# V loads on the scalar engine's DMA queue, K loads on the sync engine's

## The chip, the cores and the metric

The kernel runs on one core of a Trainium2 chip. The metric is the time of one launch in microseconds (us) of device time. A span is the time from the first to the last instruction in a profile; the launch time is about 1.7 to 1.8 us longer in every profiled run but one (198.7 against 200.4 us for the kernel before; the exception, LEAD = 1, is named below).

The engines are called PE (matmul), DVE (vector), ACT (scalar), POOL (GpSimd) and SP (sync). SP and ACT can both issue DMA transfers; SPq and ACTq in the profile are those issues.

## The reference

One step of attention with cached keys and values, one query token per sequence, over the last W = 512 positions of the cache:

```
B, D, Hq, Hkv, Sk, Dh = 32, 512, 32, 8, 2048, 128        # bf16
q = (x @ wq)                                             # 32 heads of 128
k, v = the last W = 512 positions of k_cache, v_cache, each of the 8 kv heads repeated 4 times
p = softmax(q k^T * Dh**-0.5)
out = (p v) @ wo                                         # [32, 1, 512]
```

Bytes: K and V are 33.55 MB each, wq and wo 4.19 MB each; together 75.5 MB. The unit of this document is a *batch*: the K, or the V, of one sequence is 1.05 MB, loaded as two transfers of 512 KB.

## The kernel before

All loads are issued by SP, so they go through one queue, in this order (shortened):

```python
NK = 6; NV = 8; LEAD = 5; PVLAG = 6
# SP
x, then wq in 4 pieces
for b in range(B + LEAD):
    if b < B:
        load_k(b)            # waits until the K buffer of batch b-6 was transposed
    if b >= LEAD:
        load_v(b - LEAD)     # waits until PV of batch b-LEAD-8 is done
sp.wait_ge(pe_qt, 1)         # wo takes the place of wq
wo in 4 pieces of 8 heads
# ...
```

PE does, at step `it`: the 32 transposes of K(it), the scores of batch it-1, and PV (probabilities times V) of batch it-6. After every fourth batch there is a softmax: max on DVE, exp on ACT, normalising on DVE, transposes of P on PE, copies of them on ACT. ACT also copies a quarter of each transposed K. At the end comes the output projection, piece by piece as wo lands:

```python
pe.wait_ge(dve_oT, B)                       # all 32 PV results copied
for hq in range(HQ):
    c = hq % 4
    if hq % 8 == 0:
        pe.wait_ge(sem_wo[hq // 8], 16)
    ins = pe.matmul(KT_ps[:, c, :].bitcast(F32)[32 * c:32 * (c + 1), :],
                    lhsT=oT_sb[:, :, hq], rhs=wo_sb[:, hq, :], ...)
# then DVE and ACT copy the four partial sums, one matmul adds them, ACT copies, SP stores
```

Of the kernel before, what the change touches and what calls it, by code (L numbers as in the profile page):

```python
# [7 lines left out]
ACTF = mybir.ActivationFunctionType  # L8
# [4 lines left out]
def bass_standalone__sliding_block_cached__sampling_kernel(  # L13
# [7 lines left out]
):  # L21
    B, Sq, D = x.shape
    _, HKV, SK, DH = k_cache.shape
    HD = wq.shape[1]
    HQ = HD // DH
# [12 lines left out]
    NV = 8  # L38
    NKT = 3
    NQB = 8  # L40
    LEAD = 5
# [3 lines left out]
    with ExitStack() as es:  # L45
        sb = lambda name, shape, dt: es.enter_context(nc.sbuf_tensor(name, shape, dt))
        ps = lambda name, shape, dt: es.enter_context(nc.psum_tensor(name, shape, dt))
        sem = lambda name: es.enter_context(nc.semaphore(name))
# [5 lines left out]
        V_sb = sb("V_sb", [P, NV, 2, NR, DH], BF16)  # L54
# [18 lines left out]
        junk = sb("junk", [P, 2], F32)  # L73
# [10 lines left out]
        sem_v = [sem(f"sem_v{i}") for i in range(NV)]  # L84
# [6 lines left out]
        pe_PV = sem("pe_PV")  # L91
# [17 lines left out]
        act_PT = sem("act_PT")  # L109
        act_out = sem("act_out")  # L110
        act_warm = sem("act_warm")
        pool_init = sem("pool_init")
        pool_qbd = sem("pool_qbd")
        block = es.enter_context(nc.Block())
# [4 lines left out]
        def cache_rows(cache, b, h):  # L119
            return cache[b, 4 * h:4 * h + 4, SK - W:, :].rearrange("g (s r) d -> s g (r d)", s=NS)  # L120

        @block.sync
        def _(sp):
            sp.dma_start(x_sb[:, :], x.rearrange("b s d -> b (s d)")).then_inc(sem_x, 16)
            for kt in range(DKT):
                sp.dma_start(wq_sb[:, kt, :], wq[kt * P:(kt + 1) * P, :]).then_inc(sem_wq[kt], 16)  # L126

            def load_k(b):
                if b >= NK:
                    sp.wait_ge(pe_T[3], b - NK + 1)  # L130
                for h in range(2):
                    sp.dma_start(  # L132
                        K_sb[:, b % NK, h].rearrange("p r d -> p (r d)"), cache_rows(k_cache, b, h)
                    ).then_inc(sem_k[b % NK][h], 16)

            def load_v(b):
                if b >= NV:
                    sp.wait_ge(pe_PV, b - NV + 1)
                for h in range(2):
                    sp.dma_start(  # L140
                        V_sb[:, b % NV, h].rearrange("p r d -> p (r d)"), cache_rows(v_cache, b, h)
                    ).then_inc(sem_v[b % NV], 16)

            for b in range(B + LEAD):
                if b < B:
                    load_k(b)
                if b >= LEAD:
                    load_v(b - LEAD)
            sp.wait_ge(pe_qt, 1)
            for c in range(4):  # L150
                sp.dma_start(  # L151
                    wo_sb[:, c * 8:(c + 1) * 8, :],
                    wo[c * 1024:(c + 1) * 1024, :].rearrange("(h d) n -> d h n", d=P),
                ).then_inc(sem_wo[c], 16)
            sp.wait_ge(act_out, 1)
            sp.dma_start(out.rearrange("b s d -> b (s d)"), out_sb[:, :]).then_inc(sem_out, 16)
            sp.wait_ge(sem_out, 16)
# [228 lines left out]
        @block.scalar  # L386
        def _(act):
            act.wait_ge(pool_init, 3)
            act.activation(junk[:, 1:2], junk[:, 0:1], ACTF.Exp).then_inc(act_warm, 1)
            act.wait_ge(pe_qt, 1)  # L390
            act.activation(
                QT_sb[:, 16:32, :].rearrange("p h b -> p (h b)"), PT_ps[:, 1, :].bitcast(F32), ACTF.Copy
            ).then_inc(act_qt, 1)

            def kt_evac(b):
                if b >= NKT:
                    act.wait_ge(pe_S, b - NKT + 1)
                act.wait_ge(pe_T[3], b + 1)
                act.activation(  # L399
                    KT_sb[:, b % NKT, 1, 8:16, :, :], KT_ps[:, 3, :], ACTF.Copy  # L400
                ).then_inc(act_T, 1)

            def do_exp(q):
                act.wait_ge(dve_sm, 2 * q + 2)
                if q >= 1:
                    act.wait_ge(dve_P, 4 * q)
                act.activation(  # L407
                    P_f32[:, :], S_ps[:, :], ACTF.Exp,
                    bias=negmax[:, q:q + 1], scale=SCALE, accum_out=sums[:, q:q + 1],
                ).then_inc(act_exp, 1)  # L410

            def pt_evac(q):
                if q >= 2:
                    act.wait_ge(pe_PV, 4 * (q - 2) + 4)
                for i in range(2):
                    act.wait_ge(pe_PT, 2 * q + i + 1)
                    act.activation(  # L417
                        PT_sb[:, q % 2, 8 * i:8 * i + 8, :].rearrange("p r n -> p (r n)"),
                        PT_ps[:, i, :], ACTF.Copy,
                    ).then_inc(act_PT, 1)  # L420

            for it in range(B + 2):
                if it < B:
                    kt_evac(it)
                if it % 4 == 0 and 4 <= it:
                    do_exp((it - 4) // 4)
                if it % 4 == 1 and 5 <= it:
                    pt_evac((it - 5) // 4)
            act.wait_ge(pe_fin, 1)
            for c in range(2, 4):  # L430
                act.activation(
                    X_sb[32 * c:32 * (c + 1), :], KT_ps[:, c, :].bitcast(F32)[32 * c:32 * (c + 1), :], ACTF.Copy
                ).then_inc(act_x, 1)
            act.wait_ge(pe_out, 1)
            act.activation(out_sb[:, :], QO_ps[0:32, :], ACTF.Copy).then_inc(act_out, 1)
# [28 lines left out]
```

## Time and profile before

| | before |
|---|---|
| time, median of 4 runs | 200.36 us (200.28 to 200.49) |
| span of the profiled run | 198.7 us |
| DMA rate, 20 to 160 us (table of windows) | 408 GB/s |
| K(31) has landed, its last transposes start | 166.05 us |
| last copy of a PV result ends | 183.84 us |
| last piece of wo has landed, its matmuls start | 192.86 us |

These lines are from the page of the kernel before: the span; the busy time of each engine; two rows of the table of 40 slices of 5 us (DMA busy in tenths, GB/s); the one data queue with its share of the 16 DMA engines; the chain of waits by engine; and three kinds of issue, with the median time from issue to landing at the end of the line.

```profile
span 198.7 us, 5891 instructions
...
PE 142.8 (72%) x2597; PEld 111.8 (56%) x2597; DVE 100.8 (51%) x188; ACT 58.3 (29%) x70; POOL 13.3 (7%) x46
...
DMA  5999999999999999999999999999999999999930
GB/s 181 424 418 411 409 407 412 403 411 407 408 411 403 409 407 407 410 407 409 406 407 410 407 413 403 408 407 407 411 406 411 401 409 406 410 396 334 344 133 7
...
q1 hardware_dynamic: 23264, 75.57, 96.6%
...
SPq 50%; DMA 28%; PE 14%; DVE 3%; issue 2%; ACT 1%; DVEq 0%
...
K_sb<-in_k_cache_dram SPq DMA_DIRECT2D x64, 512.0 KB, 15.6
V_sb<-in_v_cache_dram SPq DMA_DIRECT2D x64, 512.0 KB, 15.4
...
w_sb<-in_wo_dram SPq DMA_DIRECT2D x4, 1024.0 KB, 17.6
```

The transfers bound the kernel. From the second slice to the 35th they run at some 400 to 425 GB/s and the DMA row shows 9 tenths, while PE is busy 72% and DVE 51%. The chain is made of SP's issues and of landings. A transfer lands 15.6 us after its issue (median) because others are in front of it: 11 in the median had been issued and had not landed.

These lines are from the timeline of the last 35 us: start, duration, engine, line, operation, output and inputs, count, and in brackets the idle time before it and what ended that.

```profile
166.05 1.75 PE L236 MATMUL KT_ps<-perm,K_sb 128*128 128x128 bf16 x16 [0.35 <-DMA K_sb<-in_k_cache_dram]
...
183.65 0.19 DVE L366 CAST oT_sb<-QO_ps 128x32 bf16<-128x32 f32 x1 [1.11 <-PE QO_ps L286]
...
184.35 1.07 PE L308 MATMUL KT_ps<-w_sb,oT_sb 128*32 128x512 bf16 x8 [0.73 <-DMA w_sb<-in_wo_dram]
...
192.86 1.08 PE L308 MATMUL KT_ps<-w_sb,oT_sb 128*32 128x512 bf16 x8 [1.61 <-DMA w_sb<-in_wo_dram]
193.99 1.20 ACT L431 ACTIVATE X_sb<-KT_ps 32x512 bf16<-32x512 f32 x2 [15.38 <-PE KT_ps L308]
194.00 1.39 DVE L382 CAST X_sb<-KT_ps 32x512 bf16<-32x512 f32 x2 [10.15 <-PE KT_ps L308]
...
196.72 0.36 SPq L156 DMA_DIRECT2D out_dram<-out_sb  x1
```

There are two chains at the end. One is the *compute tail*: K(31) lands at 166.05 us, and 17.8 us later, at 183.84 us, the last PV result has been copied. The other is the *load tail*: V(27..31) and wo, still in the queue, keep landing until 192.86 us. The second ends later, so it sets the time; PE waits for each piece of wo. After it, a matmul group of 1.08 us and the copies, the adding matmul and the store end the span, 5.8 us in all.

### The profile page before, as it was taken

The page shows a single profiled execution, that of the slowest core. Times are in us where ns is not written, and L with a number is a line of the kernel's source. Part 1 is how long each engine was busy: PE and PEld are TensorE (multiplying, and loading weights), DVE is VectorE, ACT ScalarE, POOL GpSimd, SP SyncE. Part 2 cuts the span into 40 slices and gives each one's busy share as a digit, 9 for nine tenths or more (in the row PEclk, how much of TensorE's full clock was granted, in tenths as well). Part 3 has the DMA queues.
Part 4 walks back from the last instruction along what each step waited for, and adds up shares of the span by engine and source line. Part 5 has one row for each costly group of instructions (what it writes and reads, how often), then busy time and mean ns, then how long its engine had stood idle before and what let it go on. Part 6 is the DMA issues. An engine that isn't in the chain of part 4 may idle for free.

```text
span 198.7 us, 5891 instructions
## 1 busy us (share of the span) xinstructions
PE 142.8 (72%) x2597; PEld 111.8 (56%) x2597; DVE 100.8 (51%) x188; ACT 58.3 (29%) x70; POOL 13.3 (7%) x46
## 2 busy tenths in 40 slices
PE   0448996797787799759776977697769697647431
PEld 0337874776565568556755666566656485537000
DVE  0004579755853577335943595359435944531002
ACT  2001345333252325204522343233423251130003
POOL 8202000000000001000000000000000000000000
PEclk9999999699999969988998799969996797855555
DMA  5999999999999999999999999999999999999930
GB/s 181 424 418 411 409 407 412 403 411 407 408 411 403 409 407 407 410 407 409 406 407 410 407 413 403 408 407 407 411 406 411 401 409 406 410 396 334 344 133 7
DMA packets 23289, 75.95 MB, mean 382 GB/s; under 512 B 2208, under 2 KB 6368, under 8 KB 22752
## 3 DMA queue, kind: packets, MB, share of 16 engines
q1 hardware_dynamic: 23264, 75.57, 96.6%
q8 instruction: 21, 0.34, 0.7%
q14 instruction: 4, 0.03, 0.0%
HBM read 75.53 MB, written 0.03 MB: 380 GB/s over the span
## 4 chain that ended last, share of the span: by engine, by line
SPq 50%; DMA 28%; PE 14%; DVE 3%; issue 2%; ACT 1%; DVEq 0%
SPq L132 24%; DMA K_sb<-in_k_cache_dram 23%; SPq L140 18%; PE KT_ps L236 9%; SPq L151 7%; DMA w_sb<-in_wo_dram 6%; PE S_ps L253 2%; DVE P_ex L359 2%; PE QO_ps L286 1%; SPq L126 1%; DVE KT_sb L337 1%; PE PT_ps L268 1%; PE KT_ps L308 1%; ACT P_f L407 0%; DVEq L45 0%
## 5 line engine op out<-in xcount | busy, mean ns | idle before, releaser
L236 PE MATMUL KT_ps<-perm,K_sb 128*128 128x128 bf16 x1024 | 75.8, 238 | 22.6 <-DMA K_sb<-in_k_cache_dram 22.4
L337 DVE COPY KT_sb<-KT_ps 128x1024 bf16<-128x1024 bf16 x96 | 63.7, 687 | 53.2 <-PE KT_ps L236 52.9
L236 PEld LDWEIGHTS KT_ps<-perm,K_sb 128*128 128x128 bf16 x1024 | 67.0, 107 | 29.2 <-DMA K_sb<-in_k_cache_dram 26.7
L399 ACT ACTIVATE KT_sb<-KT_ps 128x1024 bf16<-128x1024 bf16 x32 | 32.8, 1024 | 83.0 <-PE KT_ps L236 83.0
L286 PEld LDWEIGHTS QO_ps<-PT_sb,V_sb 128*128 128x128 bf16 x1024 | 28.2, 98 | 17.4 <-issue 13.9
L286 PE MATMUL QO_ps<-PT_sb,V_sb 128*128 128x16 bf16 x1024 | 31.2, 171 | 2.4 <-ACT PT_sb L417 1.2
L359 DVE TENSOR_SCALAR P_ex<-P_f,recip 32x512 bf16<-32x512 f32 x32 | 25.3, 791 | 1.1
L253 PE MATMUL S_ps<-KT_sb,QBD 128*32 128x512 bf16 x256 | 22.7, 437 | 0.0
L417 ACT ACTIVATE PT_sb<-PT_ps 128x1024 bf16<-128x1024 bf16 x16 | 15.5, 1021 | 19.1 <-PE PT_ps L268 19.1
L268 PE MATMUL PT_ps<-ident,P_ex 128*128 128x128 bf16 x128 | 9.7, 236 | 10.6 <-DVE P_ex L359 10.6
L196 POOL COPY QBD<-QT_sb 128x32 bf16<-128x32 bf16 x32 | 7.9, 261 | 117.6 <-PE S_ps L253 108.6
L268 PEld LDWEIGHTS PT_ps<-ident,P_ex 128*128 128x128 bf16 x128 | 8.2, 106 | 11.5 <-DVE P_ex L359 11.5
L366 DVE CAST oT_sb<-QO_ps 128x32 bf16<-128x32 f32 x32 | 5.9, 183 | 9.5 <-PE QO_ps L286 9.4
L214 PE MATMUL PT_ps<-xT_sb,w_sb 128*128 128x32 bf16 x128 | 4.1, 188 | 7.6 <-DMA w_sb<-in_wq_dram 7.6
L308 PE MATMUL KT_ps<-w_sb,oT_sb 128*32 128x512 bf16 x32 | 4.3, 637 | 6.0 <-DMA w_sb<-in_wo_dram 6.0
L214 PEld LDWEIGHTS PT_ps<-xT_sb,w_sb 128*128 128x128 bf16 x128 | 3.7, 104 | 8.0 <-DMA w_sb<-in_wq_dram 4.6
L343 DVE TENSOR_REDUCE maxv<-S_ps 128x1 f32<-128x512 f32 x8 | 5.5, 691 | 5.2 <-PE S_ps L253 5.2
L407 ACT ACTIVATE P_f<-S_ps,negmax 128x512 f32<-128x512 f32 x8 | 5.5, 688 | 6.8 <-DVE negmax L345 6.8
L382 DVE CAST X_sb<-KT_ps 32x512 bf16<-32x512 f32 x2 | 1.4, 680 | 10.2 <-PE KT_ps L308 10.2
L329 DVE CAST QT_sb<-PT_ps 128x512 bf16<-128x512 f32 x1 | 0.7, 692 | 11.5 <-PE PT_ps L214 11.5
L253 PEld LDWEIGHTS S_ps<-KT_sb,QBD 128*32 128x32 bf16 x256 | 4.0, 97 | 4.0 <-issue 1.6
L308 PEld LDWEIGHTS KT_ps<-w_sb,oT_sb 128*32 128x32 bf16 x32 | 0.9, 149 | 8.7 <-DMA w_sb<-in_wo_dram 7.9
(27 smaller groups left out, 15.2 us busy)
## 6 DMA issues: line engine op xcount, KB each, us to landing
K_sb<-in_k_cache_dram SPq DMA_DIRECT2D x64, 512.0 KB, 15.6
V_sb<-in_v_cache_dram SPq DMA_DIRECT2D x64, 512.0 KB, 15.4
w_sb<-in_wq_dram SPq DMA_DIRECT2D x4, 1024.0 KB, 7.9
w_sb<-in_wo_dram SPq DMA_DIRECT2D x4, 1024.0 KB, 17.6
x_sb<-in_x_dram SPq DMA_DIRECT2D x1, 32.0 KB, 1.7
out_dram<-out_sb SPq DMA_DIRECT2D x1, 32.0 KB, 1.5
```

The lines of the kernel that those rows point to most:

```text
L132: sp.dma_start(K_sb[:, b % NK, h].rearrange("p r d -> p (r d)"), cache_rows(k_cache, b, h)).then_inc(sem_k[b % NK][h], 16)
L140: sp.dma_start(V_sb[:, b % NV, h].rearrange("p r d -> p (r d)"), cache_rows(v_cache, b, h)).then_inc(sem_v[b % NV], 16)
L151: sp.dma_start(wo_sb[:, c * 8:(c + 1) * 8, :], wo[c * 1024:(c + 1) * 1024, :].rearrange("(h d) n -> d h n", d=P),).then_inc(sem_wo[c], 16)
L196: pool.tensor_copy(dst, src).then_inc(pool_qbd, 1)
L236: ins = pe.matmul(KT_ps[:, t, i * 128:(i + 1) * 128], lhsT=K_sb[:, b % NK, h, 8 * (t % 2) + i, :], rhs=perm[:, :, :], start=True, stop=Tru ...
L253: ins = pe.matmul(S_ps[32 * c:32 * c + 32, :], lhsT=QBD[:, b % NQB, g, :], rhs=KT_sb[:, b % NKT, h, :, c, :], start=(j == 0 and h == 0), s ...
L268: ins = pe.matmul(PT_ps[:, r // 8, (r % 8) * 128:(r % 8 + 1) * 128], lhsT=P_ex[:, r, :, :].rearrange("p s g -> p (s g)"), rhs=ident[:, :], ...
L286: ins = pe.matmul(QO_ps[:, 16 * h:16 * h + 16], lhsT=V_sb[:, b % NV, h, r, :], rhs=PT_sb[:, q % 2, r, :].rearrange("p (c n) -> p c n", c=G ...
L337: dve.tensor_copy(KT_sb[:, b % NKT, t // 2, 8 * (t % 2):8 * (t % 2) + 8, :, :], KT_ps[:, t, :]).then_inc(dve_T, 1)
L359: dve.tensor_scalar(P_ex[rows, :, :, c], P_f32[rows, :].rearrange("p (r s) -> p r s", r=NR), recip[rows, q:q + 1], None, op0=ALU.mult,).th ...
L399: act.activation(KT_sb[:, b % NKT, 1, 8:16, :, :], KT_ps[:, 3, :], ACTF.Copy).then_inc(act_T, 1)
L417: act.activation(PT_sb[:, q % 2, 8 * i:8 * i + 8, :].rearrange("p r n -> p (r n)"), PT_ps[:, i, :], ACTF.Copy,).then_inc(act_PT, 1)
```

## The change

The intent is to spread the issues over two queues: SP issues K, ACT issues V, so that neither waits for the other's buffers. The core of the diff:

```diff
-            def load_v(b):
-                ...                                # on SP
-            for b in range(B + LEAD):
-                if b < B:
-                    load_k(b)
-                if b >= LEAD:
-                    load_v(b - LEAD)
+            for b in range(B):
+                load_k(b)
             sp.wait_ge(pe_qt, 1)
+            sp.wait_ge(act_v, 1)                   # wo after the last V was issued
...
+            def load_v(b):                         # on ACT
+                if b >= NV:
+                    act.wait_ge(pe_PV, b - NV + 1)
+                for h in range(2):
+                    act.dma_start(
+                        V_sb[:, b % NV, h].rearrange("p r d -> p (r d)"), cache_rows(v_cache, b, h)
+                    ).then_inc(sem_v[b % NV], 16)
+            load_v(0)
             for it in range(B + 2):
+                if it + 1 < B:
+                    load_v(it + 1)
+                if it == B - 1:
+                    act.activation(junk..., ACTF.Copy).then_inc(act_v, 1)
                 if it < B:
                     kt_evac(it)
```

(Cut: the declaration of `act_v`, and a wait for ACT's own first exp.) Nothing is computed differently and no byte more is moved. What changes besides the issuing engine is the *order*: LEAD, which held V five batches behind K, is gone.

More of the change, by code (lines that the diff above doesn't have):

```diff
@@ L111, in bass_standalone__sliding_block_cached__sampling_kernel @@
         act_warm = sem("act_warm")
+        act_v = sem("act_v")
         pool_init = sem("pool_init")
@@ L134, in load_k @@
                     ).then_inc(sem_k[b % NK][h], 16)
-            def load_v(b):
-                if b >= NV:
-                    sp.wait_ge(pe_PV, b - NV + 1)
-                for h in range(2):
-                    sp.dma_start(
-                        V_sb[:, b % NV, h].rearrange("p r d -> p (r d)"), cache_rows(v_cache, b, h)
-                    ).then_inc(sem_v[b % NV], 16)
-            for b in range(B + LEAD):
-                if b < B:
-                    load_k(b)
-                if b >= LEAD:
-                    load_v(b - LEAD)
+            for b in range(B):
+                load_k(b)
             sp.wait_ge(pe_qt, 1)
+            sp.wait_ge(act_v, 1)
             for c in range(4):
@@ L389, in _ @@
             act.activation(junk[:, 1:2], junk[:, 0:1], ACTF.Exp).then_inc(act_warm, 1)
+            act.wait_ge(act_warm, 1)
             act.wait_ge(pe_qt, 1)
@@ L420, in pt_evac @@
                     ).then_inc(act_PT, 1)
+            def load_v(b):
[6 more added lines that the diff above has]
+            load_v(0)
             for it in range(B + 2):
+                if it + 1 < B:
+                    load_v(it + 1)
+                if it == B - 1:
+                    act.activation(junk[:, 0:1], junk[:, 1:2], ACTF.Copy).then_inc(act_v, 1)
                 if it < B:
```

## The prediction

> **What bounds the kernel now.** The transfers. The slice table shows DMA at 9 tenths from slice 2 to slice 38 and 403 to 413 GB/s in almost every slice from 4 to 34; the page counts 75.95 MB, and the chain of waits is 50% sync-queue issues and 28% DMA. PE is busy 72%, DVE 51%, ACT 29%. PE waits for K tiles before most transposes (49.1 us in the view of K_sb). One queue carries everything in first-in first-out order: K runs LEAD = 5 batches ahead of V, so K(31) is followed by V(27..31) and by wo. In the timeline K(31) has landed at 166.05 us; from there to the last PV copy at 183.84 us is a compute tail of 17.8 us (transposes, scores, softmax, P transposes, four PV steps). It is hidden, because V(27..31) and wo keep the queue busy until about 192.86 us, when the last wo piece lands. From the last wo matmul group's end (193.94) to the end of the span (198.66) are 4.7 us.
>
> **What the change does.**
> - Issue cost. An unblocked 512 KB issue took 0.60 us on the sync queue (the first K issues, 4.1 to 8.7 us); later ones took 1.08 us and up to 3.7 us because about 12 transfers were outstanding (median 15.6 us to landing). That blocking is backpressure, not lost bandwidth, so freeing SP saves nothing. ACT gains about 1.25 us of issue per batch; with 1.02 us of KT copy and about 0.7 us of exp and PT copies (per batch) it has some 3 us of work in a period of 5.13 us (2.10 MB at 409 GB/s). ACT should not become the limit.
> - Bandwidth. The Trainium skill, "DMA: Bandwidth & Descriptors", section "Issuing engines are not separate DMA queues", says both run on the same 16 engines and only issue time is saved. No trace here has two data queues, so it is untested; I expect 405 to 415 GB/s again.
> - Order. The same page, "Queues, rings and completion order", says each engine round-robins between queues by packet. Both streams have 4 KB packets, so while both have work K gets half. V(it+1) is issued when ACT has copied batch it-1, so V is no longer five batches behind K but level with it. This is the change that matters.
>
> **Cost.** Before, K(31) landed after wq 4 + K 32 + V(0..25) 26 = 62 MiB. After, about 31.5 MiB of V precede it: 67.5 MiB, 5.5 MiB = 5.8 MB more, at 407 GB/s 14.2 us later: about 180 us. wo then needs about 12.5 us (334 GB/s in the last slices) and lands near 194. But the compute tail now starts at 180: the last PV copy at about 198, then four wo matmul groups back to back without DMA waits (0.5 + 4 x 1.08 us), then 4.7 us: span about 207.5, time about 209 us. DMA ends before the compute and idles some 10 us at the end. All of the roughly 9 us lies on the critical path; nothing is gained elsewhere.
>
> **What would show it.** Two data queues of about 36 MB each; K landing about 25 to 30 us after issue, V about 8 to 12; DMA rate unchanged; K(31)'s transposes near 180 us; wo matmuls without waits for wo; chain ending through softmax and PV rather than through wo.
>
> **What would make it wrong.** Unequal sharing: if K gets more than half, V lags and K(31) lands earlier (one batch less V saves 2.6 us, at best the old time). Two queues moving bytes faster or slower by 2% (3.5 us either way). ACT blocked by its issues or by waits for PV, delaying KT copies (slower still). V starvation late in the run.
>
> Predicted 209 us, 203 to 214; faster 0.04, same 0.16, slower 0.80.

## The result

| | before | after |
|---|---|---|
| time, median of 4 runs | 200.36 us | 203.19 us (202.91 to 203.54) |
| ratio | | 1.0142 (1.0123 to 1.0161) |
| span of the profiled run | 198.7 us | 201.2 us |
| DMA rate, 20 to 160 us | 408 GB/s | 408 GB/s |
| last transposes of K(31) start | 166.05 us | 176.59 us |
| last PV copy ends | 183.84 us | 193.21 us |
| last piece of wo has landed | 192.8 us | 193.0 us |

A ratio here is the mean time of one kernel's fast runs over that of the other's in the same rounds, so it is not quite the ratio of the medians. The changed kernel is slower by 1.4%: well outside the noise, and less than 2%. The landings are from the trace's completion events.

The same lines of the page after the change:

```profile
span 201.2 us, 5894 instructions
...
PE 142.7 (71%) x2597; PEld 112.4 (56%) x2597; DVE 101.7 (51%) x188; ACT 58.5 (29%) x71; POOL 13.0 (6%) x46
...
DMA  5999999999999999999999999999999999999800
GB/s 191 417 421 409 408 407 409 411 406 411 406 411 406 412 402 405 411 406 415 402 413 405 408 409 409 409 406 407 412 404 406 411 406 410 388 366 349 292 18 7
...
q1 hardware_dynamic: 14048, 42.01, 53.6%
q10 hardware_dynamic: 9216, 33.56, 41.9%
...
DMA 76%; PE 11%; SPq 6%; DVE 3%; ACT 2%; issue 1%; DVEq 0%; ACTq 0%
...
K_sb<-in_k_cache_dram SPq DMA_DIRECT2D x64, 512.0 KB, 27.0
V_sb<-in_v_cache_dram ACTq DMA_DIRECT2D x64, 512.0 KB, 16.4
...
w_sb<-in_wo_dram SPq DMA_DIRECT2D x4, 1024.0 KB, 11.9
```

The busy times are nearly the same (ACT is at 29% as before) and so is the rate. There are two data queues: SP's (q1), with K and the weights, and ACT's (q10), with V. A K transfer now takes 27.0 us from issue to landing instead of 15.6, because it gets only half of the rate. The chain of waits is no longer issues of SP but landings of K.

The timeline of the end, after:

```profile
176.59 1.07 PE L227 MATMUL KT_ps<-perm,K_sb 128*128 128x128 bf16 x16 [0.46 <-DMA K_sb<-in_k_cache_dram]
...
193.02 0.19 DVE L357 CAST oT_sb<-QO_ps 128x32 bf16<-128x32 f32 x1 [1.11 <-PE QO_ps L277]
...
193.26 3.15 PE L299 MATMUL KT_ps<-w_sb,oT_sb 128*32 128x512 bf16 x32 [0.28 <-DVE oT_sb L357]
...
196.47 1.39 DVE L373 CAST X_sb<-KT_ps 32x512 bf16<-32x512 f32 x2 [3.26 <-PE KT_ps L299]
...
198.99 0.36 SPq L147 DMA_DIRECT2D out_dram<-out_sb  x1
```

The load tail has not moved: wo has landed at 193.0 us. The compute tail has: it starts 10.5 us later and now ends after the load tail. So the 32 matmuls with wo, which before were spread over the waits for wo, stand behind the last PV copy in one group of 3.15 us; no wait for wo is left. They end at 196.41 us instead of 193.94, which is the 2.5 us by which the span grew.

### The profile page after: what moved, and what is told of

Read it like the earlier page. It is cut to its first block, busy times and chain, and to the rows that moved or that the text cites. A ratio compares the mean times of both kernels' runs of the same rounds, so it can differ in the third digit from the quotient of the medians.

```text
span 201.2 us, 5894 instructions
## 1 busy us (share of the span) xinstructions
PE 142.7 (71%) x2597; PEld 112.4 (56%) x2597; DVE 101.7 (51%) x188; ACT 58.5 (29%) x71; POOL 13.0 (6%) x46
## 4 chain that ended last, share of the span: by engine, by line
DMA 76%; PE 11%; SPq 6%; DVE 3%; ACT 2%; issue 1%; DVEq 0%; ACTq 0%
DMA K_sb<-in_k_cache_dram 76%; PE KT_ps L227 5%; SPq L133 5%; PE QO_ps L277 3%; PE KT_ps L299 2%; DVE P_ex L350 2%; SPq L127 1%; ACT PT_sb L409 1%; PE S_ps L244 1%; PE PT_ps L259 1%; DVE oT_sb L357 0%; ACT P_f L399 0%; DVEq L45 0%; DVE maxv L334 0%; DVE X_sb L373 0%
## 5 line engine op out<-in xcount | busy, mean ns | idle before, releaser
L227 PE MATMUL KT_ps<-perm,K_sb 128*128 128x128 bf16 x1024 | 77.1, 238 | 33.5 <-DMA K_sb<-in_k_cache_dram 33.0
L328 DVE COPY KT_sb<-KT_ps 128x1024 bf16<-128x1024 bf16 x96 | 64.5, 688 | 61.7 <-PE KT_ps L227 61.3
L277 PEld LDWEIGHTS QO_ps<-PT_sb,V_sb 128*128 128x128 bf16 x1024 | 28.4, 99 | 17.8 <-issue 14.3
L277 PE MATMUL QO_ps<-PT_sb,V_sb 128*128 128x16 bf16 x1024 | 31.3, 171 | 2.4 <-ACT PT_sb L409 1.2
L244 PE MATMUL S_ps<-KT_sb,QBD 128*32 128x512 bf16 x256 | 23.5, 451 | 0.0
L383 ACT ACTIVATE QT_sb<-PT_ps 128x512 bf16<-128x512 f32 x1 | 0.6, 598 | 12.3 <-PE PT_ps L205 12.3
L436 ACT ACTIVATE X_sb<-KT_ps 32x512 bf16<-32x512 f32 x2 | 1.2, 590 | 8.5 <-PE KT_ps L299 8.5
L299 PE MATMUL KT_ps<-w_sb,oT_sb 128*32 128x512 bf16 x32 | 3.2, 562 | 0.3 <-DVE oT_sb L357 0.3
## 6 DMA issues: line engine op xcount, KB each, us to landing
V_sb<-in_v_cache_dram ACTq DMA_DIRECT2D x64, 512.0 KB, 16.4
```

The source lines that it names most:

```text
L227: ins = pe.matmul(KT_ps[:, t, i * 128:(i + 1) * 128], lhsT=K_sb[:, b % NK, h, 8 * (t % 2) + i, :], rhs=perm[:, :, :], start=True, stop=Tru ...
L244: ins = pe.matmul(S_ps[32 * c:32 * c + 32, :], lhsT=QBD[:, b % NQB, g, :], rhs=KT_sb[:, b % NKT, h, :, c, :], start=(j == 0 and h == 0), s ...
L277: ins = pe.matmul(QO_ps[:, 16 * h:16 * h + 16], lhsT=V_sb[:, b % NV, h, r, :], rhs=PT_sb[:, q % 2, r, :].rearrange("p (c n) -> p c n", c=G ...
L328: dve.tensor_copy(KT_sb[:, b % NKT, t // 2, 8 * (t % 2):8 * (t % 2) + 8, :, :], KT_ps[:, t, :]).then_inc(dve_T, 1)
```

## The experiments

Theory A: what counts is how far K is ahead of V in the bytes moved. It fixes when K(31) lands and so when the compute tail starts; the compute tail costs time only where it ends later than the load tail. Which engine issues is of no account. Rival B: the V issues on ACT delay the copies of K. Rival C: two data queues disturb each other.

### Two queues, V later: act_lag and act_late

```diff
# act_lag: against the changed kernel
-            load_v(0)
             for it in range(B + 2):
-                if it + 1 < B:
-                    load_v(it + 1)
+                if 1 <= it <= B:
+                    load_v(it - 1)
...
             sp.wait_ge(act_v, 1)
+            sp.wait_ge(sem_v[29 % NV], 32 * (29 // NV + 1))    # wo after V(29) has landed

# act_late: against the changed kernel
+            act.wait_ge(sem_k[2][1], 16)                       # K(2) has landed
             load_v(0)
```

> V stays on the scalar queue with the same issues, but two batches later: V(b-1) instead of V(b+1) at the scalar engine's step b; wo is held until V(29) has landed, so that it does not take half the rate from V at the end. Theory A (what counts is how many batches of V have been moved when K(31) lands, whichever queue moves them): V starts to flow near 24 us instead of 18.7, K(31) lands at 165 to 170 us instead of 176.5, the last PV copy is over before 190 us, and the time is that of the kernel before, 200.4 +- 0.8 us. Theory B (issues on the scalar engine, 1.2 us per batch, slow the copies): 203 us as in the changed kernel. Theory C (two data queues disturb each other): 203 us as well.

> The changed kernel with one wait more: the scalar engine waits for K(2) to land before it issues V(0); from then on every V(b+1) is issued at the same program step as in the changed kernel. Theory A with a conserved lead (both queues always have work and share equally, so the lead that K has when V starts lasts to the end): V starts to flow about 4 to 5 us later, K's lead grows by about one batch or more and K(31) lands about 3 to 5 us earlier, 172 to 174 us; time 200.4 to 201.5 us. Rival A2 (the program step at which V is issued sets the lead): K(31) lands again at 176.5 us, time 203 us or more, because the first KT copy starts 5 us later.

| | time, median | ratio to before | K(31) has landed | last PV copy ends |
|---|---|---|---|---|
| changed kernel | 203.19 us | 1.0142 | 176.5 us | 193.21 us |
| act_lag | 200.86 us (200.09 to 201.23) | 1.0032 (1.0016 to 1.0049) | 172.1 us | 188.74 us |
| act_late | 200.64 us (200.57 to 201.06) | 1.0014 (0.9999 to 1.0029) | 169.1 us | 186.97 us |

With every V issue still on ACT and both queues in use, the loss is gone, or all but 0.3% of it. So B and C fall as explanations of the 1.4%. The traces say the same of B directly. In the changed kernel all the idle time of ACT before its copies of K was ended by PE's transposes, and each of the 32 copies started 0.1 us after them, as in the kernel before. In act_late, which is faster, ACT was held up by its V issues: the copies started 1.8 us after the transposes in the mean, and PE waited for them; the load tail hid it. The first line is from the page of the changed kernel, the second from that of act_late (busy us, mean ns, idle us before and what ended most of it):

```profile
L391 ACT ACTIVATE KT_sb<-KT_ps 128x1024 bf16<-128x1024 bf16 x32 | 32.8, 1025 | 94.9 <-PE KT_ps L227 94.9
...
L227 PE MATMUL KT_ps<-perm,K_sb 128*128 128x128 bf16 x1024 | 81.0, 248 | 15.6 <-ACT KT_sb L391 13.5
```

The end of the chain of waits of act_late (start, duration, what) shows the load tail in charge again, as in the kernel before:

```profile
180.94 11.82 DMA w_sb<-in_wo_dram
...
192.80 1.11 PE KT_ps L299 x8
```

Both landing times of K(31) missed what I had expected, one late (172.1, expected 165 to 170), one early (169.1, expected 172 to 174). The packet records of the two queues say why. The table counts batches moved on each queue, K with the weights taken off:

| | first V packet | K ahead of V at 30 us | at 90 us | at 150 us | V moved when K(31) landed |
|---|---|---|---|---|---|
| changed kernel | 18.7 us | 2.4 | 2.4 | 2.4 | 31.3 |
| act_lag | 23.3 us | 4.1 | 4.1 | 4.1 | 29.6 |
| act_late | 26.5 us | 5.3 | 5.3 | 5.3 | 28.5 |

The lead that K has when V's first packet moves stays to a tenth of a batch until K runs out. That is what the Trainium skill's "DMA: Bandwidth & Descriptors", section "Queues, rings and completion order", leads one to expect: each engine takes packets from the queues that have work in turn. For the changed kernel, the DMA view of 40 to 150 us has these two lines (packets, MB, share of the 16 engines):

```profile
q1 hardware_dynamic: 6126, 22.31, 50.9%
q10 hardware_dynamic: 6129, 22.33, 50.9%
```

An equal share keeps a difference; it does not close one. The program step at which V is issued does not set the lead, as long as the V queue never runs dry: act_late issues every V at the same step as the changed kernel, and keeps the head start that its one wait at the beginning gave to K. Its V transfers just stand in their queue longer, 26.1 us from issue to landing against 16.4:

```profile
V_sb<-in_v_cache_dram ACTq DMA_DIRECT2D x64, 512.0 KB, 26.1
```

### One queue, V closer: sp_lead3, sp_lead2, sp_lead1, sp_lead0

The other half of the proof is the kernel before, with nothing on ACT and one queue, and one number changed:

```diff
-    LEAD = 5
+    LEAD = 1        # and 3, 2, 0 in the other three
```

> The kernel before with V 3 batches behind K instead of 5, one queue. Slack theory: K(31) lands two batches of V later, near 171.2 us, the last PV copy ends near 188.5 us, still before the last piece of wo has landed (192.8), so the delay is hidden: 200.4 +- 0.5 us. A rival that charges every batch of order with its 2.6 us, as my prediction nearly did: 205 us; one that spreads the measured 2.5 us for four batches evenly: 201.7 us.

> V 2 batches behind K. Slack theory: K(31) near 173.7 us, the last PV copy near 191 us, right at the point where the slack ends (about 190.5 us): 200.4 to 201.3 us. Even spread of the loss over the batches: 202.3 us.

> The kernel before with one number changed: V runs 1 batch behind K instead of 5, all on the one sync queue; nothing issued on the scalar engine. Theory A: K(31) lands four batches of V later, 166.0 + 4 x 2.57 = 176.3 us, the last PV copy ends near 193 us, time 203 us, as the changed kernel. Theories B and C: no scalar issues and no second queue, so 200.4 us.

> As sp_lead1, with V directly behind the K of its own batch. Theory A: K(31) lands near 178.9 us and, the slack being used up, one batch more of V costs its whole 2.6 us: 205.6 us. Theories B and C: 200.4 us.

| | K(31) has landed | moved by then besides K and wq | last PV copy ends | time, median | ratio to before |
|---|---|---|---|---|---|
| LEAD = 5 (before) | 166.0 us | 27.3 batches | 183.84 us | 200.36 us | 1 |
| LEAD = 3 | 171.2 us | 29.2 | 187.84 us | 200.34 us | 0.9995 (0.9981 to 1.0008) |
| LEAD = 2 | 173.8 us | 30.3 | 190.42 us | 200.36 us | 0.9993 (0.9978 to 1.0009) |
| LEAD = 1 | 176.3 us | 31.3 | 194.23 us | 202.98 us | 1.0141 (1.0088 to 1.0193) |
| LEAD = 0 | 179.1 us | 32.2 (some wo in it) | 195.79 us | 205.51 us | 1.0253 (1.0235 to 1.0272) |

LEAD = 1 loses what the changed kernel loses, 1.0141 against 1.0142, without a second queue and without one issue on ACT. That the two agree so closely is luck: the runs of LEAD = 1 lie between 202.23 and 204.91 us, and the highest, the profiled one, is 3.0 us above its span of 201.9 us where the others are 1.8 us above theirs. V moved 31.3 batches by the landing of K(31) in both. Its timeline ends the same way, with one undivided group of 32 matmuls behind the last PV copy:

```profile
176.32 1.89 PE L236 MATMUL KT_ps<-perm,K_sb 128*128 128x128 bf16 x16 [0.21 <-DMA K_sb<-in_k_cache_dram]
...
194.04 0.19 DVE L366 CAST oT_sb<-QO_ps 128x32 bf16<-128x32 f32 x1 [1.11 <-PE QO_ps L286]
...
194.29 3.13 PE L308 MATMUL KT_ps<-w_sb,oT_sb 128*32 128x512 bf16 x32 [0.28 <-DVE oT_sb L366]
```

The row of times is flat and then rises, as a hidden cost does when its cover is used up. The cover can be worked out from the profile before: the load tail ends its matmuls at 193.94 us, and the undivided group takes 3.15 us, so a last PV copy that ends before about 190.7 us costs nothing. LEAD = 2 is just at this point: its copy ends at 190.42 us, one undivided group follows it and ends at 194.11 us (3.64 us, at a granted clock of 0.50 where the changed kernel had 0.60), and its time is still that of the kernel before. Before the change 6.9 us of this cover were unused. The change moved the copy by 9.4 us, to 193.21: 2.5 us too far.

### A shorter path after the last landing: tail

If the load tail sets the time of the kernel before, then what stands behind the last landing is worth shortening, and this helps where the order of loads cannot.

```diff
+    WO = [0, 12, 20, 28, 32]           # pieces of wo in heads; before: 0, 8, 16, 24, 32
...
-                if hq % 8 == 0:
-                    pe.wait_ge(sem_wo[hq // 8], 16)
+                if hq in WO:
+                    pe.wait_ge(sem_wo[WO.index(hq)], 16)
...
-                    KT_ps[:, c, :].bitcast(F32)[32 * c:32 * (c + 1), :],
+                    KT_ps[:, 0, :].bitcast(F32)[32 * c:32 * (c + 1), :],
...
-            (DVE copies c = 0, 1 and ACT copies c = 2, 3, each 32x512)
+            dve.tensor_copy(X_sb[:, :], KT_ps[:, 0, :].bitcast(F32)).then_inc(dve_x, 1)
```

(Cut: the loads of wo in these pieces, and PE's waits for the copies.)

> The kernel before with its order of loads, and a shorter path after the last landing of wo: the last piece of wo is 4 heads instead of 8 (pieces of 12, 8, 8, 4), and the four partial sums of the output projection share one PSUM bank, so that one 128x512 copy of about 0.69 us replaces two copies of 32x512 one after the other (1.39 us). If the end is the landing of wo plus this path, it saves about 0.5 us of matmul and 0.7 us of copy: 199.2 +- 0.4 us. If the end is set elsewhere: 200.4 us.

Measured: 199.31 us (199.16 to 199.63), ratio 0.9946 (0.9934 to 0.9959). It is the fastest kernel here, 0.5% under the kernel before and 1.9% under the changed one (199.31 and 203.19, medians of different rounds). Its timeline after the last landing:

```profile
192.68 0.65 PE L310 MATMUL KT_ps<-w_sb,oT_sb 128*32 128x512 bf16 x4 [0.30 <-DMA w_sb<-in_wo_dram]
193.38 0.69 DVE L382 CAST X_sb<-KT_ps 128x512 bf16<-128x512 f32 x1 [10.82 <-PE KT_ps L310]
...
195.46 0.36 SPq L158 DMA_DIRECT2D out_dram<-out_sb  x1
```

The last group takes 0.65 us instead of 1.08 and one copy takes 0.69 us where there were two after one another, 1.39 us. That is 1.1 us of the 1.3 by which the span fell (198.7 to 197.4); the last piece also landed 0.2 us earlier. The order of the loads is that of the kernel before; what is issued where was not touched.

All seven experiments gave the reference's result.

## Why the prediction was wrong

It forecast 209 us, slower by over 2% with a chance of 0.80. The time was 203.19: right in direction, on the edge of the range, and the loss is a third of the forecast (2.8 us, forecast 8.6). The mechanism held and its sizes did not. Point by point:

- *The transfers bound the kernel, and a second queue adds no bandwidth*: right. 408 GB/s in both. The skill's "Issuing engines are not separate DMA queues" (in "DMA: Bandwidth & Descriptors") says that issuing from several engines "will only save the time on the sequencer it takes to initiate the DMA"; the rate agrees with it. As a statement about this kernel's time it is not enough, since the order of the landings changed with the queue.
- *ACT does not become the limit*: right. Its issues took 0.62 us in the median and ran beside its copies; these two lines of the timeline start together:

```profile
19.69 1.02 ACT L391 ACTIVATE KT_sb<-KT_ps 128x1024 bf16<-128x1024 bf16 x1 [4.38 <-PE KT_ps L227]
19.70 1.45 ACTq L418 DMA_DIRECT2D V_sb<-in_v_cache_dram  x2
```

- *V is no longer five batches behind K, each queue gets half, K(31) lands later, the compute tail becomes the end, wo is no longer waited for, nothing is gained elsewhere*: right, each shown by a line above and turned off and on by the experiments.
- *V "level with" K*, and so *"about 31.5 MiB of V precede it"*: this is the step that failed. K kept a lead of 2.4 batches, so by their places in the queues 32 - 2.4 = 29.6 batches of V go before the end of K. Against the 26 before, counted in the same way, that is 3.6 batches more, not 5.5. The first V was issued at 14.73 us but its first packet moved at 18.7 us, when K was already 2.3 batches ahead. The DMA view of 14 to 18.6 us has four V issues and not one packet of queue 10:

```profile
q1 hardware_dynamic: 516, 1.86, 101.0%
q8 instruction: 1, 0.02, 1.4%
issues: line engine op xcount, KB each, median us to landing
V_sb<-in_v_cache_dram ACTq DMA_DIRECT2D x4, 512.0 KB, 10.8
```

- *"Before, K(31) landed after ... V(0..25) 26 = 62 MiB. After, about 31.5 MiB of V precede it ... 5.5 MiB = 5.8 MB more, at 407 GB/s 14.2 us later: about 180 us"*: moved by the landing of K(31) were 27.3 batches of V before and 31.3 after, more than the 26 and 29.6 that go ahead of it. That 31.3 is close to the 31.5 forecast is luck: the lead that was left out and the surplus of 1.7 nearly cancel. The surplus is there because landing does not follow the order of issue strictly: 16 of the 32 completion events of V(26), issued behind K(31), had come by 165.5 us, the last of K(31) at 166.0. In the LEAD series it is the same every time, 1.2 to 1.3 batches (LEAD = 1: 30 issued ahead, 31.3 moved), so it drops out when like is compared with like. The real difference is 4.0 batches = 4.2 MB, 10.3 us at 408 GB/s; measured, 10.5 us from 166.05 to 176.59. The trace supports a reason for the surplus. A landing is counted by 16 completion events; those of the second half of K(31) came from 161.37 to 166.01 us before, and from 170.28 to 176.54 us after, in the mean 2.7 and 4.0 us ahead of the last. If each is the event of one of the 16 DMA engines, which no record here states, most engines were done with K early and went on with V: by estimate 1.0 and 1.6 batches at 408 GB/s, of the 1.3 and 1.7 counted.
- *The compute tail takes 17.8 us again*: it took 16.6 us (176.59 to 193.21). In the kernel before, the 16 last transposes took 1.75 us and the scores of the batch before 1.04 us, at a granted clock of 0.55 and 0.50 (table of windows); here they took 1.07 and 0.61, at 1.00. LEAD = 1 had 0.50 in both, and a tail of 17.9 us, which accounts for its last copy ending 1.0 us after that of the changed kernel; LEAD = 3, 2 and 0 had 1.00, and 16.6 us.
- *"0.5 + 4 x 1.08 us" for the matmuls with wo*: 3.20 us. Back to back, 32 of them take 3.15 us, not four times the 1.08 us of a group of eight. The clock has a part in this: it was 0.50 in the groups of eight and 0.60 here. LEAD = 0 had 0.50, and its 32 took 3.64 us.

Put together: forecast span 207.5 us; 3.4 us less for the landing of K(31), 1.4 less for the compute tail from 180 to 198, 1.6 less for the matmuls with wo give 201.1; the span was 201.2. These errors are of some 10 to 30% of their terms. They became a factor of three because the loss is a small difference: 9.4 us of delay less 6.9 us of cover.

Two smaller misses: the queues carried 42.0 and 33.6 MB, not 36 each, since the weights stay with K (a slip in adding); and V took 16.4 us to land, not 8 to 12, since six of its transfers (three batches) in the median, and up to seven, were in front of a new one.

One thing stays open. act_lag is slower than the kernel before by 0.3% with an interval that excludes 0, though its compute tail ends within the cover. Even the size is unsure: the means of all runs differ by 0.2%, and the profiled run is the fastest of its five (200.09 us; the others 200.82 to 201.23). Its chain of waits goes through the landing of a V and the issues of wo that were held for V(29), so this added wait is a candidate; no run here tests it.

## What to carry to other kernels

When the transfers are the bound, look at a move of loads to another queue as a change of their order; the rate stayed at 408 GB/s here. Find out which load gates the longest chain of work at the end, and keep it early. With an equal share, and as long as neither queue runs dry, the head start that one stream gets at the beginning lasts until it ends, so one wait before the first load of the other stream sets it. Where two chains end close together, compute the cover first: a delay costs only what exceeds it, and an estimate of the loss is only as good as the difference of the two.

## What the Trainium skill lacked or had wrong

- "DMA: Bandwidth & Descriptors", "Queues, rings and completion order": the round robin by packet holds (22.31 and 22.33 MB in 110 us), but what follows from it for two streams is not said: a lead is kept (2.4, 4.1 and 5.3 batches, constant from 30 to 150 us).
- The same page, "Latency and other measured facts", gives about 600 ns to the first byte for this kind of DMA. On a second queue, with the DMA engines busy for the first, the first packet moved 3.9 to 4.1 us after the start of the issue (14.7 to 18.7, 19.2 to 23.3, 22.5 to 26.5 us). On SP's queue at the start, with nothing in front, it took 1.0 us (0.74 to 1.75).
- The same page, "Issuing engines are not separate DMA queues", says that only issue time is saved. It lacks the warning that the order of landings changes with the queue; here that cost 1.4%.
- No page that I read says how much of a transfer issued later on the same queue moves before an earlier one has landed; here it was 1.2 to 1.3 batches of 1.05 MB.
